# A conformer block on one core: whole chunks instead of half chunks behind the last exponential, and a newly searched order

## The chip, the cores and the metric

The kernel runs on one core of one Trainium2 chip. The metric is the time of one execution in device microseconds (us); lower is better. TensorE multiplies matrices, ScalarE evaluates activations, VectorE does elementwise work and reductions, GpSimd small elementwise work, and SyncE (SP) issues DMAs, as does ScalarE's queue now and then.

## What is computed

Two sequences of 4000 tokens with 144 features, bfloat16, go through one block. `_layernorm` has no weights.

```python
h = _layernorm(x); h = _silu(h @ w_ff1a) @ w_ff1b; x = x + 0.5 * h      # 144 -> 576 -> 144
h = _layernorm(x); qkv = h @ w_qkv                                       # 4 heads of 36
scores = jnp.einsum('bhqd,bhkd->bhqk', q, k) * scale; p = _softmax(scores)
x = x + (p @ v, heads merged) @ w_o
h = _layernorm(x) @ w_pw1; a, b = h[..., :D], h[..., D:]; h = a * _sigmoid(b)
c = depthwise convolution of h over tokens, 5 taps, w = dw
x = x + _silu(c) @ w_pw2
h = _layernorm(x); h = _silu(h @ w_ff2a) @ w_ff2b; x = x + 0.5 * h
return _layernorm(x)
```

The attention is over all 4000 tokens of a sequence: 2 x 4 x 4000 x 4000 exponentials. The rest is linear in the tokens.

## The kernel before

**Tiling.** The 8000 tokens are 16 chunks of 500, chunks 0 to 7 being the first sequence; a chunk is four blocks of 125 tokens. The keys of a chunk's queries are walked in tiles of 64 (63 per sequence, the last one of 32 rows). One item is one key tile for one chunk and all four heads: 16 x 63 = 1008 items. TensorE makes the scores in four 64x64 quadrants into two PSUM banks, an engine takes the exponential into a tile `PT`, and TensorE multiplies `PT` with the values `VA` (37 columns, the last one of ones, so that the sums come along). `TYPES` says per item who takes the exponential: `A` ScalarE in one instruction of 1000 columns, `D` VectorE in two of 500 by integer arithmetic on the bits and three more steps, `W` the same with one first instruction of 1000 columns, `R` the short last tile on ScalarE.

**Stages of a chunk.** `pre` is the first feed-forward and the projections. `epilogue` normalises the attention's sums into `AN`. `post1` transposes `AN`, adds the projection by `w_o`, and makes layer norm and gated unit (`U`). `post2` makes the convolution (`conv`, `conv_left`) with its SiLU (`SW`), the projection by `w_pw2`, a layer norm with transposes (`ln_tr`), the second feed-forward (`ff` for whole chunks, `ff_part` for half ones), the last layer norm and the store (`store`, which calls `ln` and issues the DMA to `out`).

**Half and whole chunks.** The function `small(c)` says whether chunk `c` goes in halves of two blocks:

```python
def small(c):
    return mode["tail"] or mode["front"] and c < FULL
def parts(c):
    return [range(0, 2), range(2, 4)] if small(c) else [range(0, 4)]
```

`mode["tail"]` is switched on when all items' exponentials and sums have been planned; the stages planned behind that point are called the tail here. They are `post1` of chunk 15 and `post2` of chunks 11 to 15. In `ln_tr` a half chunk is transposed by TensorE (four transposes of 125 columns for two blocks into a PSUM bank, then `copy` to `XTB`), a whole one by one DMA transpose that SP issues (`dma_transp`). In `ln`, a half chunk takes its variance step on VectorE by default, the power of -0.5 on GpSimd over 2 columns and the normalisation `XN` on VectorE or ScalarE; a whole one takes variance, power over 4 columns and `XN` on GpSimd by default. In the tail the SiLU is one activation on ScalarE: for a half chunk two of 500 columns (two tiles of 250 each) and one of 250, for a whole one four of 500 and one of 250. Chunks 14 and 15 share the convolution's seam at their end (`glu_end`, `conv_end`), which works on halves.

**The order.** A planner (`Sched`, `pick`, and in the tail a loop that takes the thread with the earliest start, shifted by `TJ`; `FLEX` shifts the choice of engine for copies) makes a list of steps. Its order is not the one that runs. `settle` and `arrange` put each engine's steps into the order of the table `ORDER` (steps numbered per engine, two letters each), and take the PSUM banks, the `PT` buffers and the places of the other PSUM tiles from `BANKS`, `SLOTS` and `PLACES`. `UNITS` holds one letter for each choice of engine among VectorE (`d`), GpSimd (`p`) and ScalarE (`a`), in the planner's order: copies, the variance step, the `XN` steps of a layer norm, and residual additions (on ScalarE these need two more matmuls with an identity). 465 letters before; the first 377 are planned ahead of the tail, and the first 106 of them within the front, where the first sequence's keys are made. Each engine runs its own list in order, and waits where a step needs another engine's result. All instructions are issued by one helper, so every row of the profile has its line, L591.

Of the kernel before, what the change touches and what calls it, by code (L numbers as in the profile page):

```python
# [13 lines left out]
H = 4  # L14
# [21 lines left out]
        '!!!#!$!%!&!(!)!*!+!,!-!.!/!0!1!2!5!4!7!3!6!<!8!9!=!:)n)o!;!>)r)s!?)v)w)z){!@!A*!*#!B!C*&*(!D*,*+!E!F'  # L36
        '!K!G!H!I!N!J!L!M!Q!S!R*$*.)|)u*))q*-)})x*%)p)y)t!V!T!W!U!P!b!O!`!^!X!Y!Z!_!j!a![!h!i!c!d!g!f!l!e!k!]'
        '*0*/!o!m*4*3!n!p*8*7*2***<*;!q*?*@*6*5*D*C*1*:!r!s*H*G!u*L*K!t!w!v*E*F*P*O*T*S!x!y*B*M*W*X!z*J*I*A*]'
        '*b*c*9*N*[*Q*>*f*g!{*k*j*Y*R!|!}*n*o###!*r*_*y*x*s*p*e*=*}*^*|*V*U*q#$#%#&+-+%+$*Z*a*z*v+.*{+)+**`*h'
        '*i*d+7+8#(+3+4*u+&#)+F+++2*t*l*w+;+<#*+E+(+#+!*m+?+0+/+I+J+:+Q+1+,+9+@+M+N+G+=+>#,#++R+W+X+O+]+L+P+6'  # L40
        '+[#-+`+f+C+g+K+5+D+_+a+^+k+j+Z+A#.+n+o+B+U+H+Y+V+v+r+s+T+S+|+}#/,%,$+m+l+i+u+t,),*+w+h,#,!+p,.,-#0,2'
        ',1#1,<,;+q,/+e+d,5,0,?,@,6+b+c,3,4+z,D,C#2,G,H,B,>,=,R,&,Q+{,K,F,+,L+y,E,U,V,J,A,:+x,,,I,Z,Y,_,S,9,^'
        ',T#3,c,b,8,7,W,X,f,(,l,m#4,p,q,[,g,d,P,e,M,t,u#5#6,y,x,],O,a,|-&-(#7-,-+,k,v,N,j,},r-0-/#8-4-3-.,z,w'
        ',`-7,{-=->#9-A-B-8-)-2-5---*-F-E-6-I,h,s-J-1#:-C-M-N,o,n-D-H-Q-R-V-U,i-K-G-<-]-[-$-@-!-%-`-a-O-e-d-P'
        '-9-#-j-k-T-S-L-;-:-?-o-n#=-r-s#;#<#?#@#>-v-w-Z-Y-{.&-z-_-^-c-l-u-m-b.!.##A#B#C.(-t...-#D.2.1.$.%-q-p'
        '-W-X.5.6#E-y.=-x.0.9.:#F.C.D.3.8./.4.7.>.H.G#G.K.L-f.<.,.;.+-i.P.O#H-|.S.T.X.N.W.F-g.M.?.Q.].E.R.[.V'
        '.A.@.`.c.*.B.i.j.Z.Y.m.n-}.I-h.J.^._.d.U.r.q.).b.a.u.v#I/#/$#J.p/(.o.f/).y.h.k/,/-/%.t#K.z/0.x.e.s/1'
        '/4.g/5/+/&.w.l/*/8///?/>#L/B/C.}/!/2/9/./F/G#M/J/K#N/U/T/N/E/I/H/A/6/D/Y/X/7/3/@/O/L.|#O/^/]/M/V/Z/b'
        '/a/=.{/W#P/j/</i/[/f/R/e/S/;/_/o#Q/y/x/`/|/:/}/g#R0$0%/Q/k/l/c/d/r0/00/m/n/s/P0304/h0)/q/p0=0>#S070A'
        '0B02010E0!0(0F08050&0#/z0*0O0P0C0@0?/{060I0T0S0G0H#T0W0X0D0Q0R0J0[0]#U0`0a0Y#V0d0e0^0Z0_/v0<0;0o0n/w'  # L50
        '0b090V0U0:0r0s/t0c/u0h0w0f0g0v#W0{0z0p0M0q0K0i1!1#0.0L0t0N0x1&1(#Y#X1+1,0-0,0|0}1%1/1$0u1)10#Z191:1-'
        '1*0y130m0+1=1>#[1B1A1.0l140j1F1E#]1I1J#^1N1M#_1U1R1H1Q1G1D17111]1[120k1C1?1V1<151;1`1a#`#a161O1e1S1Z'
        '1d1Y1_1@1W1i1h181^1l1X1m1s1r1L1T1K1b1c1v1w#b2%2$1z1k1f1g2*2)#c2.2-1n2(1j1{27281q2&2,211o2;2<1P201p22'
        '2?2@#d2+2J2I291y1u1t2C2#2/2B2>2M2N2:1|#e2Q2R2L2D2O1x2P2]2[262!2V2=2a2`242U1}2S2T2d2e#f2i2^2c2h2b2K2_'
        '2H2l2m232A#g2F2w2E2p2k2q252j2x#h2t3!2}2Z2n2r2Y2W2X3&3%2g3.2s2G2f3/3*3+2o2v2u3534#k#j39383,3-3=3<#i3A'
        '3@373(3)2{3;3L3E3D3M3:363?3H3I3#2|2y2z3B333R3S#l3V3W3F3G3>3$3K3_3[3Z3J3`3T3O323f3e313P3U303i3j3Y3q#m'
        '3n3]3m3N3r3x3k3w3l3^3C3h3X4(3Q3|3{#n3o4$4#433p3c3y4/3u3d4.3g3z3}4!423v4B4)#o#p48493b4<3s4&4M4%4L413a'
# [2435 lines left out]
```

## Time and profile before

| | |
|---|---|
| time, median of 3 runs | 875.51 us (875.36 to 875.64) |
| profiled execution, its own time | 875.88 us |
| its span, first to last instruction | 874.0 us |
| granted TensorE clock, mean | 0.998 |
| end of the last exponential | about 825.7 us of the span |

A profile row of a group has its engine, operation, output and inputs, shapes, count, busy time and mean duration; then the idle time of the engine just before such instructions and what ended it. A matmul's duration includes the latency of its pipeline, so that matmuls overlap; the time from one start to the next says how fast they go. A window's row has busy time by engine (count of instructions), then the granted clock.

### The profile page before, as it was taken

The numbers are of one execution on the slowest core, as the hardware profiler recorded it, in microseconds if no ns is written. First come the engines' busy times: TensorE is split into PE (matmuls) and PEld (weight loads), VectorE is DVE, ScalarE is ACT, GpSimd is POOL, SyncE is SP. The second block draws the span as 40 slices with busy tenths as digits, with TensorE's granted clock in tenths as the row PEclk, the third lists the DMA queues.
The fourth block names the chain that finished last, engine by engine and source line by source line (L and its number), as shares of the span: only waits on it lengthen the run. The fifth ranks groups of instructions, "written<-read, shape, count | busy, mean of one in ns | idle before, by whom it ended". The sixth has DMA issues, their size and how long they took to land.

```text
span 874.0 us, 27149 instructions
## 1 busy us (share of the span) xinstructions
PE 855.2 (98%) x11637; PEld 413.3 (47%) x11637; DVE 843.6 (97%) x1853; ACT 839.0 (96%) x1101; POOL 283.4 (32%) x540
## 2 busy tenths in 40 slices
PE   9999999999999999999999999999999999999996
PEld 7643434444344444434444444444545444444586
DVE  7999999999999999999999999999999999999987
ACT  7899999999999999999999999999999999999975
POOL 6760341031514302511330241210541260501645
PEclk9999999999999999999999999999999999999999
DMA  3230111102112101211310010101120021000201
GB/s 101 65 74 4 33 20 38 33 14 44 21 38 43 34 14 21 45 25 26 33 38 1 9 38 9 26 14 14 26 51 5 18 44 26 19 16 14 42 19 40
DMA packets 83552, 26.12 MB, mean 30 GB/s; under 512 B 78231, under 2 KB 83432, under 8 KB 83432
## 3 DMA queue, kind: packets, MB, share of 16 engines
q1 hardware_dynamic: 81884, 23.70, 14.2%
q8 instruction: 91, 1.49, 0.7%
q10 hardware_dynamic: 1548, 0.69, 0.3%
q14 instruction: 29, 0.24, 0.1%
HBM read 3.31 MB, written 2.30 MB: 6 GB/s over the span
## 4 chain that ended last, share of the span: by engine, by line
PE 43%; ACT 38%; DVE 16%; DMA 1%; issue 1%; POOL 1%; DVEq 0%; POOLq 0%; ACTq 0%
PE PS L591 43%; ACT PT L591 35%; DVE PT L591 11%; ACT TH L591 3%; DVE ST L591 1%; DMA XTB<-XN 1%; DVE U L591 1%; DVE X L591 1%; DVE XN L591 1%; DVE HT L591 0%; DVE QT L591 0%; DVE SW L591 0%; POOL XN L591 0%; DVE AN L591 0%; ACT KT L591 0%
## 5 line engine op out<-in xcount | busy, mean ns | idle before, releaser
L591 ACT ACTIVATE PT<-PS 128x1000 bf16<-128x1000 f32 (+1 forms) x793 | 731.4, 1071 | 6.2 <-PE PS L591 4.8
L591 PE MATMUL PS<-QT,KT 64*64 64x500 bf16 x3968 | 455.8, 383 | 4.3 <-ACT PT L591 1.2
L591 PE MATMUL PS<-PT,VA 64*37 64x500 bf16 x4828 | 451.9, 372 | 1.8 <-DVE QT L591 0.9
L591 DVE TENSOR_SCALAR PT<-PS 128x500 int16<-128x500 f32 (+1 forms) x424 | 279.9, 678 | 4.5 <-PE PS L591 2.5
L591 PEld LDWEIGHTS PS<-QT,KT 64*64 64x64 bf16 x3968 | 138.4, 104 | 203.8 <-ACT PT L591 103.3
L591 PEld LDWEIGHTS PS<-PT,VA 64*37 64x37 bf16 x4828 | 162.8, 96 | 107.1 <-DVE PT L591 15.0
L591 POOL TENSOR_SCALAR RS<-ST 125x4 f32<-125x4 f32 (+1 forms) x118 | 31.3, 266 | 484.6 <-DVE ST L591 480.2
L591 DVE TENSOR_SCALAR PT<-PT 128x1000 uint16<-128x1000 uint16 x430 | 171.5, 415 | 1.7 <-PE PS L591 0.5
L591 DVE TENSOR_TENSOR PT<-PT 128x1000 bf16<-128x1000 bf16 x215 | 145.4, 679 | 1.1
L591 POOL TENSOR_SCALAR XN<-X,RS 125x144 bf16<-125x144 bf16 x236 | 134.9, 585 | 3.9 <-DMA out_dram<-XN 0.3
L591 POOL TENSOR_TENSOR RS<-RS,NHALF 125x4 f32<-125x4 f32 (+2 forms) x99 | 97.0, 983 | 70.0 <-DVE RS L591 67.8
L591 ACT ACTIVATE TH<-PS 128x500 bf16<-128x500 f32 (+3 forms) x175 | 94.5, 564 | 3.4 <-PE PS L591 2.9
L591 DVE SCALAR_TENSOR_TENSOR HT<-TH,PS 128x500 bf16<-128x500 bf16 (+1 forms) x120 | 71.7, 614 | 1.8 <-ACT TH L591 1.0
L591 PE MATMUL PS<-XTB,WA 72*128 72x500 bf16 (+2 forms) x304 | 72.3, 344 | 0.5
L591 DVE BATCH_NORM_STATS2 ST<-X 125x6 f32<-125x288 bf16 (+1 forms) x160 | 66.2, 447 | 2.0 <-DMA X<-in_x_dram 1.1
L591 DVE SCALAR_TENSOR_TENSOR X<-PS,X 125x288 bf16<-125x288 f32 (+1 forms) x112 | 50.0, 450 | 4.1 <-PE PS L591 3.2
L591 PE MATMUL PS<-WB,HT 128*125 128x144 bf16 (+1 forms) x640 | 51.9, 229 | 0.1
L591 PEld LDWEIGHTS PS<-WB,HT 128*125 128x125 bf16 (+1 forms) x640 | 44.8, 136 | 12.7 <-issue 3.6
L591 PEld LDWEIGHTS PS<-XTB,WA 72*128 72x128 bf16 x304 | 23.0, 97 | 27.8 <-issue 9.5
L591 PE MATMUL PS<-U,DG 128*128 128x375 bf16 (+5 forms) x204 | 27.9, 263 | 0.1
L591 ACT ACTIVATE HT<-PS 128x500 bf16<-128x500 f32 (+3 forms) x46 | 21.4, 525 | 4.1 <-PE PS L591 3.6
L591 PE MATMUL PS<-IDF,QT 128*125 128x128 f32 x128 | 22.4, 298 | 0.1
(95 smaller groups left out, 525.1 us busy)
## 6 DMA issues: line engine op xcount, KB each, us to landing
X<-in_x_dram SPq DMA_DIRECT2D x16, 140.6 KB
XTQ<-XTB SPq DMA_DIRECT2D x24, 70.3 KB
out_dram<-XN SPq DMA_DIRECT2D x11, 140.6 KB
XTB<-XN SPq DMA_TRANSPOSE x50, 3.1
out_dram<-XN SPq DMA_DIRECT2D x6, 70.3 KB
XTB<-AN SPq DMA_TRANSPOSE x15, 3.1
out_dram<-XN ACTq DMA_DIRECT2D x3, 70.3 KB
WA<-in_w_ff1a_dram ACTq DMA_DIRECT2D x1, 144.0 KB
```

What stands on the lines that cost most here:

```text
L591: ins = getattr(eng, o.name)(*o.a, **o.k)
```

## The change

`small` is true in the tail for chunks 14 and 15 alone, so `post2` of chunks 11 to 13 goes whole: transposes by DMA, `ff` in place of `ff_part`, one layer norm of four blocks where there were two of two, one store of 140 KB where there were two of 70. GpSimd's memsets of constants at the start are tied into one step (`clears`). The tables of the order are replaced, `TJ` and `FLEX` too.

```diff
+    zero = R.step
+
+    def clears(eng, dst, w, cost):
+        was = R.step
+        if eng == "pool":
+            R.step = zero
+        op(eng, "memset", dst, 0.0, w=w, cost=cost)
+        R.step = was
...
-    op("pool", "memset", WP2Z[:, :, :], 0.0, w=[("WP2Z", i) for i in range(NB)], cost=0.3)
-    op("pool", "memset", U2[:, :, :], 0.0, w=["U20"], cost=0.6)
+    clears("pool", WP2Z[:, :, :], [("WP2Z", i) for i in range(NB)], 0.3)
+    clears("pool", U2[:, :, :], ["U20"], 0.6)
...
     def small(c):
-        return mode["tail"] or mode["front"] and c < FULL
+        return mode["tail"] and c >= 14 or mode["front"] and c < FULL
...
-    FLEX = -0.2
+    FLEX = 0.8
```

The memsets of `WE1`, `WB1`, `WE2`, `WB2`, `WQ` and `WK` become `clears` in the same way; those on VectorE keep their step. The tables in numbers:

| table | before | after |
|---|---|---|
| steps of TensorE, ScalarE, VectorE, GpSimd, SP | 5060, 1093, 1721, 314, 99 | 5049, 1083, 1691, 323, 99 |
| `TYPES` A, D, W, R | 777, 209, 6, 16 | 777, 211, 4, 16 |
| `UNITS` d, p, a | 289, 118, 58 | 264, 132, 51 |

`PLACES`, `BANKS` and `SLOTS` have the same places for 1543 of some 1725 tiles, 1803 of 2016 banks and 912 of 2016 buffers. The tables' letters themselves are left out.

More of the change, by code (lines that the diff above doesn't have):

```diff
@@ L41 @@
[L41 to L45, printed above, removed]
@@ new lines @@
+    '2402403540225042502240525042504250240124120412402140204120412041240214022425055240240420542054250520'
+    '5240420342034034203420342034202430243034303430342034204330340234203402550520420424042504205240524052'
+    '5042505230524052402240524045205425042504250524052402505250525052042405240025402540523054205420452305'
+    '2340324302430134033430343024301343024302430243024302432034203423024302430041204120412041204120420402'
+    '1402041204021402041204021402041204023402140245042054250425042045240240142010524025025024012041201402'
@@ new lines @@
+    '4522500134124500234523452300452345231145234523451111543401235401235501230154230123012301223401450145'
+    '0145012245014501450145220145014532014522014501324501452201450132450145014501222401230145230123014501'
+    '3223012345012301552301235201550155440123012301230155230123540123012354012301234401340144230123012301'
+    '2344500123452355012301340124340123450134015334014501453312452201450145014533124533014501334501450133'
+    '4501450133450145330145014501220145124523004523450023452345231045234500234523004523452300452345002345'
@@ new lines @@
+    '2300452345001245234545012344012301230123440123012301235510452345230123012301234500234500234523452345'
+    '0123452345231145234523114523452311451245234510234523452301452345234511234523452311050345123422014501'
+    '3345014522014501450133450132450145220145013345014525014501323401552301442301230123012301230123540123'
+    '0123013355012301442301234401234401230144230123015523012345012301234501230123015523012345012301443401'
+    '2355012301235401230155230123012344002345234510234523004523452311452345121035234523004523452301452345'
@@ new lines @@
+    '0132450145012345014532014523134512450312450123452345234523110345124512004512452201450133451245320145'
+    '0122450145013245014501453201450145332345234500124512034512453323452311451345235423451125450145013245'
+    '0134230145124532014501235201340123451023451203450145013245014522014501234501453301450125340145014501'
+    '4512452045001423012301230123250134012301452301230155230125430101234501452301452300452345012345234523'
+    '4500231045234523450145320145123401054401234523450023452303452345123345124501134523450110452345231145'
@@ new lines @@
+    ')!#!+,*!(!%!!!()&!*!-!#!,!$&%!!!+!-!,&(!*!)!%!#!!-$!),+!,!&!!&*!(!-#$!%!(!*+#!+!%!,!$!%!),&!$!,!%!(!'
+    '&!#!!!-%+!(!*!#!$!!!,!)*&!#!(!+!#-&!%!*$,!$!!!-()!&!,!+(#!)!$!&%!!)!#!$!-!!!*!+)$!,!-!#(%!!!&!*!-!+!'
+    ',$)!&!!!*#+!%!)!(!$!&!%!,$-!#*&!(&)-%!!!&!*!+!#!!!),%!*!+!*(-!%!$!&!!-#!+!%!#!,!$!($&!%!#!*!+!-!&!#!'
+    ')!)!*+,!$!(!&!!-%!)!,!$!#!*(%!,!)!-%&!,!#!+!&!$!#!)!*!(-$!,!#%!!&!$!*!!!+!)&$!,!*,-!%!(!#+!!&!+!$!)!'
+    '-!(!&!-!,&+!%!$!%##!+!-!)!(!-!+(*!)!&!%!*($!!!,!#&-!%!&!)!+!!(,!$!*!+*%!,!$!#!-!%!&!,!(,)!-!$!*$!!)!'
@@ new lines @@
+    '-!#(&!%!+!!&$),!+!%+*!-!#!&,+!)!(!-!$!!!)+#!%!-!(!$!!!,!%(!!*!,-#!+!)!&!$!%!#!(!$*+!)!,!#!&!+!%!-!+!'
+    '#&)!*!$!%!,!(+#!)!!!#!-%$!&!,!$!*+)!%!#!$-*!&(+!!!)!%!#!$(+!-!,!!!*!)-%!!!#!(!*!&!+)$%,!-!!!*$(!#!&!'
+    ')%,!(!-!#,!!,!&!-!,!+&-!!!*,(!%!!!)$-!(!!!%-#!-!&!!$+!)!#!(+*!)!*%-!&!#(,!!!)!$!,!+!&!)!!!-!$!(&+!,!'
+    '*!$!!!-!#*%!,!$!(!!!&!)!%$+!-!(-)!+!*!&-,!#!)!$!*&#!,!+!),!!$!%!(!#!$!+!-!(!!!$-%!(!)!,#*!+!$%-+&!+!'
+    '!!#)*!(!&!)!*-%!!!$!(,+!-!$!&!!!,!#&%!+!!!)!*,(!-!%!$&)!+!#!!!(*)!,!#!)!#+&$,!(!-!),*!%!!!,!$&-!+!(!'
@@ new lines @@
+    '-!%(*!+!#!)!,+!!*!(!$%)!#!-!+)&!%!#!&%$!(!,!!!-!*!%!-!#!*!&!)+$!!!%!-!(&#!*!,!+)$!*!,!%#-!*!$!#$!!,!'
+    ')!*)&!(!+!-!!($!+!,!&!%!)*+!$!&!,!(-+!%!!!$!#&,!*!+!%!$!)!+!,&-!$!#!!*+!(-)!$!%,+!)!#!%,&!-!,!(!!+#!'
+    '$!&!*$)!#!(!+!!#-!(!)!+!&*,!-!%!)!-!,+$!(!#!!)*!(!)!%!-$+!*!#!,+&!+!$!(-!!+!*!%)$!&!(!$!*!%!#!(!&!-!'
+    ')!*!&!$%+!,!!*#!(!)!&!+!-!%-*,$!,!#!(!)!+-!!&!$!#!!)&!(!*-%&)!-!(+$!,!#!+!)$,!-!-+!!$!&!#!!!*!&!%!(!'
+    ',!*-+!%$$!&!!!+!(!&!#!!,)!+!(!)!#!-(&!&!+!*!,!%!($)!-!#!*$)!!!%!-!%!)!,!+!!!())!+!,!*!$++!#!-!&!,(-!'
@@ L299 @@
+    'ddadppdadppdddddppppdddpdppdddddadddddppadadppddddpadppdddddddpdddadppdadappddpddppddddppdppdddppddp'
+    'pdddppddpddppddappdddppdppddddppdppddppddppddppdddddppdpdddaapppdddaadppdppppddpppdddddaaddddpddddpd'
+    'pddpppdddadddaddddddddpddpddadpadddddddaddddddd'
 )
@@ L1090, in bass_standalone__conformer_family_zipformer__speech_kernel @@
     for WE, WB, nm, eng in ((WE1, WB1, "W1", "dve"), (WE2, WB2, "W2", "pool")):
-        op(eng, "memset", WE[0:HD, :, 0:64], 0.0, w=[(nm, "a", 2)], cost=0.15)
-        op(eng, "memset", WE[0:HD, :, 128:192], 0.0, w=[(nm, "a", 3)], cost=0.15)
+        clears(eng, WE[0:HD, :, 0:64], [(nm, "a", 2)], 0.15)
+        clears(eng, WE[0:HD, :, 128:192], [(nm, "a", 3)], 0.15)
         op("dve", "memset", WB[64:128, 4, :], 0.0, w=[(nm, "b", 3)], cost=0.15)
-        op(eng, "memset", WB[0:64, 5, :], 0.0, w=[(nm, "b", 4)], cost=0.15)
-    op("pool", "memset", WQ[:, :, :, :], 0.0, w=["WQ0"], cost=0.3)
-    op("pool", "memset", WK[:, :, :, :], 0.0, w=["WK0"], cost=0.3)
+        clears(eng, WB[0:64, 5, :], [(nm, "b", 4)], 0.15)
+    clears("pool", WQ[:, :, :, :], ["WQ0"], 0.3)
+    clears("pool", WK[:, :, :, :], ["WK0"], 0.3)
     op("dve", "tensor_copy", IDF[:, :], IDENT[:, :], r=["ID"], w=["IDF"], cost=0.2)
```

429 lines of the change are left out of this document (197 added, 232 removed), and 24 rows, old and new, of the table TJ.

## The prediction

> **What bounds the kernel now.** I read the page's sums first, then the busy time of each engine by stage, then the chain of waits, the timeline of TensorE, and the groups by form.
>
> ```profile
> span 874.0 us, 27149 instructions
> PE 855.2 (98%) x11637; PEld 413.3 (47%) x11637; DVE 843.6 (97%) x1853; ACT 839.0 (96%) x1101; POOL 283.4 (32%) x540
> ```
>
> Three engines look full, so the sums alone cannot say what a change is worth. The stages can. The columns are the stretch, its length, and then busy us of PE, PEld, DVE, ACT and POOL:
>
> ```profile
> 0.00:60.00 60.00, 57.54 (x707) 38.79 (x707) 53.02 (x150) 49.31 (x89) 44.20 (x91) 1.00 0.32 81
> 60.00:826.00 766.00, 757.42 (x10468) 339.51 (x10462) 751.32 (x1573) 757.73 (x942) 215.04 (x402) 1.00 0.14 25
> 826.00:866.00 40.00, 39.00 (x457) 34.03 (x456) 35.30 (x118) 30.64 (x69) 21.38 (x45) 1.00 0.14 33
> 866.00:874.00 8.00, 1.24 (x17) 0.94 (x14) 3.92 (x16) 1.35 (x3) 2.80 (x4) 0.74 0.19 54
> ```
>
> From 60 to 826 (the attention) ScalarE and VectorE carry the exponentials and leave 8.3 and 14.7 us idle. Behind the last exponential, 826 to 866, ScalarE idles 9.4 us of 40 and VectorE 4.7, but TensorE only 1.0. Its busy time is partly modelled latency, so I check the chain and the spacing of its instructions:
>
> ```profile
> 828.11 4.72 DMA XTB<-XN
> 832.83 0.05 issue
> 832.88 28.88 PE PS L591 x344
> 861.76 0.00 issue
> 861.76 2.74 PE PS L591 x34
> ...
> 868.60 1.14 DVE XN L591 x5
> ```
>
> ```profile
> 862.62 1.01 PE L591 MATMUL PS<-XTB,WA 72*128 72x250 bf16 x8
> 863.47 0.39 PE L591 MATMUL PS<-IDENT,XN 125*72 125x125 bf16 x4
> 863.70 0.79 PE L591 MATMUL PS<-WB,HT 128*125 128x144 bf16 x10
> 864.32 0.59 PE L591 MATMUL PS<-XTB,WE 72*128 72x250 bf16 x4
> ```
>
> The chain is one unbroken run of 378 matmuls, 31.6 us, behind one wait of 4.72 us for a DMA transpose. The second fence shows that it is not only latency: each group starts as the one before has streamed. Eight 250-column matmuls take 0.85 us to the next group (106 ns each), four transposes 0.23 (58 ns each), ten 144-column matmuls 0.62. So in this stage TensorE's own work sets the end, and then comes a drain of some 8 us led by VectorE and the last store.
>
> **The change, part by part.** These are the rows with the prices in the tail (826 to 874):
>
> ```profile
> L591 PE MATMUL PS<-IDENT,XN 125*72 125x125 bf16 x44 | 4.3, 218 | 0.0
> L591 PE MATMUL PS<-IDENT,XN 126*72 126x126 bf16 x4 | 0.4, 217 | 0.0
> L591 DVE COPY XTB<-PS 72x500 bf16<-72x500 bf16 x8 | 3.3, 412 | 2.5 <-PE PS L591 2.3
> L591 ACT ACTIVATE XTB<-PS 72x500 bf16<-72x500 bf16 x5 | 2.9, 585 | 0.7 <-PE PS L591 0.6
> L591 ACT ACTIVATE HT<-PS 128x500 bf16<-128x500 f32 x26 | 14.3, 585 | 2.7 <-PE PS L591 2.6
> L591 ACT ACTIVATE HT<-PS 128x250 bf16<-128x250 f32 x11 | 4.1, 379 | 1.1 <-PE PS L591 1.0
> L591 DVE TENSOR_SCALAR RS<-ST 125x2 f32<-125x2 f32 x13 | 2.1, 163 | 0.3
> L591 POOL TENSOR_TENSOR RS<-RS,NHALF 125x2 f32<-125x2 f32 x20 | 14.2, 713 | 14.3 <-DVE RS L591 13.8
> L591 POOL TENSOR_TENSOR RS<-RS,NHALF 125x4 f32<-125x4 f32 x2 | 2.1, 1049 | 0.8 <-DVE RS L591 0.8
> ```
>
> *Transposes.* 48 transposes of XN are six layer norms of 8: one in `post1` of chunk 15, one in `post2` of each of chunks 11 to 15. Going whole takes 3 x 8 = 24 from chunks 11 to 13, at 58 ns of stream: **1.4 us off TensorE**, on the chain. With them go 6 evacuations (0.41 us on VectorE or 0.59 on ScalarE, about 3.0 us together), off the chain as long as both engines have room.
>
> *Feed-forward.* A half chunk has two SiLUs of 500 columns and one of 250; two halves cost 4 x 0.585 + 2 x 0.379 = 3.10 us of ScalarE, a whole chunk 4 x 0.585 + 0.379 = 2.72. Three chunks save 1.1 us, hidden in ScalarE's 9.4 us of idle time. TensorE's columns stay (20 matmuls of 250 become 8 of 500 and 4 of 250): nothing.
>
> *Layer norms.* Each chunk has two in this stage. Whole ones need one power of 1.05 us where two of 0.71 stood, and one variance step where two of 0.163 stood. VectorE gains 6 x 0.163 = 1.0 us, GpSimd 6 x 0.38 = 2.3, both beside TensorE. VectorE leads the last 5 us of the drain, so I put 0.3 us of all its relief on the end; between nothing (these chunks are done by then) and 1.0.
>
> *DMA transposes.* SP gets three more transposes in the tail and three stores fewer (two 70 KB stores become one of 140), so its number of steps stays 99. What a transpose makes wait is seen here, behind a layer norm on GpSimd:
>
> ```profile
> 815.99 2.87 POOL L591 TENSOR_SCALAR XN<-X,RS 125x144 bf16<-125x144 bf16 x4
> 822.34 0.45 PEld L591 LDWEIGHTS PS<-XTB,WPZ 72*128 72x128 bf16 x8 [0.34 <-DMA XTB<-XN]
> 832.87 0.22 PEld L591 LDWEIGHTS PS<-XTB,WE 72*128 72x128 bf16 x3 [1.20 <-DMA XTB<-XN]
> PE PS L591 <- DMA XTB<-XN: 0.9, 1, 0.9
> ```
>
> From the last XN (818.86) to the reader's start are 3.5 us, in the chain above 4.7; TensorE stood still for 0.9 of it at 832. Queued behind such a wait is all of TensorE, in order, and behind it ScalarE's SiLUs. Three more cost between nothing (other chunks' convolutions, projections and feed-forwards fill the time, as they nearly do here) and 3 x 0.9 = 2.7 us. There are five chunks to interleave and three of them need it early, so I take 0.3. It could also gain the 0.9 that stands there now, if the new order covers it. [...]
>
> *Clears.* GpSimd's memsets are tied into one early step. They already run there, in one go, and GpSimd then waits for VectorE, so I put nothing on it; without that gap a power of 1.4 us would come later by what is left of them.
>
> ```profile
> 3.45 0.52 POOL L591 MEMSET WK<- 128x512 bf16 x1
> 5.56 1.39 POOL L591 TENSOR_TENSOR RS<-RS,NHALF 125x2 f32<-125x2 f32 x2 [1.59 <-DVE RS L591]
> ```
>
> *The order of everything else.* This is the unknown. The tables show what moves: of 1008 key tiles the kinds of 8 change, with 777 on ScalarE as before, VectorE's wide form `W` 6 to 4 and its split form `D` 209 to 211. Of the 377 choices of engine planned ahead of the tail (the first letters of `UNITS`; the first 106 belong to the front) I counted the changed letters. Beyond the front: residuals 5 each way, the copies of QT, KT and VA balanced, 6 more variance steps and one more whole XN (four steps) on GpSimd instead of VectorE.
>
> ```profile
> L591 DVE TENSOR_SCALAR PT<-PS 128x500 int16<-128x500 f32 x418 | 272.8, 670 | 4.5 <-PE PS L591 2.5
> L591 DVE TENSOR_SCALAR PT<-PS 128x1000 int16<-128x1000 f32 x6 | 7.1, 1191 | 0.0
> L591 DVE TENSOR_SCALAR XN<-X,ST,RS 125x144 bf16<-125x144 bf16 x72 | 19.6, 337 | 0.5 <-POOL RS L591 0.3
> L591 POOL TENSOR_SCALAR RS<-ST 125x4 f32<-125x4 f32 x100 | 27.4, 275 | 480.9 <-DVE ST L591 477.5
> L591 POOL TENSOR_SCALAR XN<-X,RS 125x144 bf16<-125x144 bf16 x236 | 134.9, 585 | 3.9 <-DMA out_dram<-XN 0.3
> ```
>
> VectorE: 2 x (2 x 0.670 - 1.191) = +0.3, -6 x 0.163 = -1.0, -4 x 0.337 = -1.3: together -2.0 us of 751. ScalarE: nothing. GpSimd: +6 x 0.275 + 4 x 0.585 = +4.0, with 70% of it idle. The work of this stage is the same within 0.3%; only gaps can move it. ScalarE's 8.3 us of gaps bound a gain; a loss has no such bound, and I take ScalarE's gaps at half as much again, 4.2 us, as its far end. I take -0.5, a quarter of VectorE's relief, because ScalarE is the fuller engine. For the front (TensorE 57.5 of 60) I take nothing, within 1 us either way.
>
> *Sum:* -1.4 - 0.3 + 0.3 - 0.5 = -1.9. The profiled execution took 875.88 us (span 874.0 and 1.9 around it): 874.0. The median of the runs is 0.4 lower, 875.51, so I forecast **873.6 us**, -0.22%. About 0.2% (1.75 us) is what a measurement of this kernel can tell from no change.
>
> **The rivals.**
>
> *The new order closes gaps as well.* If half of ScalarE's 8.3 us goes too, 3.6 us come on top of the 0.5 taken: 870.0. For it: VectorE is relieved and every table is new. Against it: the stage is 98.9% busy on ScalarE already.
>
> *The transposes by DMA take the gain back.* All three stall TensorE as the one at 832 does: 2.7 instead of 0.3, so 876.0, no change. Against it: the wait exists once among the many readers of that stage.
>
> *GpSimd blocks VectorE.* More steps on GpSimd may delay VectorE. VectorE's multiply of two tiles, with GpSimd nearly idle (60 to 80) and with it busy (240 to 260):
>
> ```profile
> L591 DVE TENSOR_TENSOR PT<-PT 128x1000 bf16<-128x1000 bf16 x4 | 2.7, 675 | 0.1
> L591 DVE TENSOR_TENSOR PT<-PT 128x1000 bf16<-128x1000 bf16 x5 | 3.5, 694 | 0.0
> ```
>
> 19 ns more, 3%. If VectorE stood for half of the 4.0 us that GpSimd gains, its relief of 2.0 and my 0.5 would be gone: 874.1 or, with the tail's layer norms on GpSimd too, up to 875.0. [...]
>
> *Slower: gaps on ScalarE in the attention.* TensorE's queue is in order, and a score pair that stands behind a sum still waiting for its exponential holds up the next one. Place: 60 to 826. Before, ScalarE waits little for TensorE:
>
> ```profile
> ACT PT L591 <- PE PS L591: 4.8, 20, 0.6
> ```
>
> The new sequence of TensorE has little in common with the old one (the longest common run of steps covers 32%), so these 20 waits are drawn anew. The price is that of the gaps: 4.2 us give 873.6 + 0.5 + 4.2 = 878.3. It decides once ScalarE's gaps grow by over 3.2 us (8.3 to 11.5), which eats the tail's 1.4 and leaves 1.75.
>
> **How the numbers follow.** Forecast (872.2 to 875.2): 0.52, of which 0.38 falls under 873.75 and 0.14 above. Gaps closed: 0.15. Transposes: 0.08. GpSimd: 0.05. Slower: 0.20. So faster 0.53, same 0.27, slower 0.20. The range cuts half of the slower case and little of the case of closed gaps: 869.9 to 877.9.
>
> **What would show it.** TensorE's transposes of XN by 24 fewer, DMA transposes 53 instead of 50; TensorE's run from the last exponential to its last matmul (826 to 866) shorter by 1 to 2 us; no wait of TensorE for XTB over 1 us; ScalarE's idle time from 60 to the tail within 2 us of 8.3. The prediction is wrong if the tail keeps its 48 us, or if the last exponential ends more than 2 us earlier or later.

## The result, and the profile after

The changed kernel takes **872.24 us** (median of 6 runs, 871.45 to 872.35) where the kernel before, in runs beside it, took 875.58 (6 runs, 875.07 to 876.19): a ratio of 0.9959, 95% interval 0.9946 to 0.9971, 3.3 us faster. Its profiled execution took 872.24 us, 3.64 less than that of before. The page's sums after:

```profile
span 870.4 us, 27016 instructions
PE 850.9 (98%) x11585; PEld 409.6 (47%) x11585; DVE 837.1 (96%) x1824; ACT 834.7 (96%) x1093; POOL 284.4 (33%) x562
```

(The helper that issues all instructions is line L589 in the changed kernel, and one of L589 to L593 in the kernels of the experiments.) Three engines are as full as before, so the sums again don't say where 3.6 us went. Three stretches do, cut where the last exponential ends and where the last matmul ends. The busy time by stage, first of the kernel before, then after (columns as in the prediction):

```profile
60.00:825.68 765.68, 757.10 (x10466) 339.39 (x10460) 751.00 (x1571) 757.73 (x942) 214.72 (x402) 1.00 0.14 25
825.68:867.34 41.66, 40.56 (x474) 35.09 (x470) 36.96 (x123) 31.09 (x70) 22.70 (x47) 1.00 0.14 34
867.34:874.00 6.66, 0.00 (x0) 0.00 (x0) 2.58 (x12) 0.90 (x2) 1.79 (x3) 0.69 0.17 49
```

```profile
60.00:823.49 763.49, 755.13 (x10451) 339.61 (x10448) 749.55 (x1569) 756.66 (x941) 211.87 (x414) 1.00 0.14 26
823.49:861.47 37.98, 37.98 (x431) 30.87 (x428) 32.27 (x102) 28.62 (x65) 21.98 (x43) 1.00 0.24 52
861.47:870.40 8.93, 0.00 (x0) 0.00 (x0) 3.28 (x13) 0.00 (x0) 1.71 (x2) 0.65 0.16 48
```

So the last exponential ends 2.2 us earlier (825.68 to 823.49), TensorE's stretch behind it is 3.7 us shorter (41.66 to 37.98), and the drain behind the last matmul is 2.3 us longer (6.66 to 8.93). -2.2 - 3.7 + 2.3 is -3.6, the whole difference.

**TensorE's stretch.** It was 1.10 us short of full and is now full (37.98 of 37.98), and its work has shrunk. The groups by form from 823.49 to the end, and the DMA issues:

```profile
L589 PE MATMUL PS<-IDENT,XN 125*72 125x125 bf16 x20 | 1.9, 219 | 0.0
L589 PE MATMUL PS<-IDENT,XN 126*72 126x126 bf16 x4 | 0.4, 218 | 0.0
...
XTB<-XN SPq DMA_TRANSPOSE x53, 3.2
```

Of 48 transposes by TensorE 24 are left, and three more go by DMA. The wait for a DMA transpose at 832 is gone. The two orders also divide other work differently: behind the last exponential 65 matmuls of the convolution (`PS<-U,DG`) stand where 72 stood, and 20 sums with `PT` where 6 did. What this shift is worth, beside the wait and the transposes, was not measured by itself. SP's timeline of after shows the two transposes before the tail:

```profile
819.70 1.23 SPq L589 DMA_TRANSPOSE XTB<-XN  x1
822.28 0.28 SPq L589 DMA_DIRECT2D out_dram<-XN  x1
825.44 1.23 SPq L589 DMA_TRANSPOSE XTB<-XN  x1
```

In the kernel before the last two were issued at 826.6 and 828.1 and first read at 830.8 and 832.9, with TensorE standing still for the second. Now they go 6.9 and 2.7 us earlier; the first is read at 825.2, 5.5 us behind its issue, and from 820 to 866 the view of waits has none of TensorE for `XTB`.

**The drain.** SP's and ScalarE's queues and the last windows of after:

```profile
858.07 6.09 SPq L589 DMA_DIRECT2D out_dram<-XN  x3
863.52 1.63 ACTq L589 DMA_DIRECT2D out_dram<-XN  x3
```

```profile
860.00:864.00 4.00, 1.47 (x24) 1.32 (x22) 3.53 (x13) 0.97 (x3) 2.42 (x3) 1.00 0.04 14
864.00:868.00 4.00, 0.00 (x0) 0.00 (x0) 0.85 (x4) 0.00 (x0) 0.00 (x0) 0.52 0.30 89
```

The last column is GB/s. From 860 to 864 almost nothing is moved (14, the end of an earlier store), then 89 GB/s for 4 us, which is 356 KB, and some 75 KB more in the next microsecond: two whole chunks' stores and the halves of chunk 15 (422 KB in all) land together at the very end. The last `XN` steps on VectorE, in the kernel before and in the changed one:

```profile
868.51 1.45 DVE L591 TENSOR_SCALAR XN<-X,ST,RS 125x144 bf16<-125x144 bf16 x6
862.95 1.90 DVE L589 TENSOR_SCALAR XN<-X,ST,RS 126x144 bf16<-126x144 bf16 x8
```

They are done at 869.96 and 864.85. So the drain has two parts. From the last matmul to the last `XN` it took 2.6 us and takes 3.4: a whole chunk's last norm now stands among those of the two halves. From there to the end it took 4.0 us and takes 5.5. Of the 2.3 us, 0.8 are norms and 1.5 lie behind the last norm, where only stores are left.

**Ahead of the tail.** How much of the exponentials is done by 750 us: busy time on tile `PT` alone, from 60 to 750, of ScalarE (first row) and of VectorE (second row), in the kernel before and then in the changed one:

```profile
60.00:750.00 690.00, 640.75 (x696) 1.00 0.14 26
60.00:750.00 690.00, 499.74 (x953) 1.00 0.14 26
```

```profile
60.00:750.00 690.00, 642.76 (x698) 1.00 0.15 27
60.00:750.00 690.00, 501.92 (x958) 1.00 0.15 27
```

At 750 us both engines are 2.0 and 2.2 us of exponentials ahead, about what the last exponential's end moved by. The figure depends on the cut, since other work of ScalarE stands at other places: cut at 200, 400, 600, 700 and 800 us it is 0.6, 0.3, 0.9, 1.1 and 1.3 us ahead. So the lead gathers over the attention, for the most part behind 400 us, and not at one place. The front gives none of it: by 60 us ScalarE's exponentials came to 19.91 us before and 19.74 after. From 60 us to the last exponential ScalarE runs nearly the same work in both (942 and 941 instructions), so the 2.2 us are mostly gaps: 1.1 us of idle time (765.68 - 757.73 = 7.95 to 763.49 - 756.66 = 6.83), and 1.1 us of busy time. Overlapping instructions count once in it (in the kernel before, one of ScalarE's ends at 807.61 and the next starts at 807.38), so closer starts can show as less busy time; how much of the 1.1 us is that, and how much the one instruction less, was not taken apart.

### The profile page after: what moved, and what is told of

The parts are those of the page before. It is cut to its first block, busy times and chain, and to the rows that moved or that the text cites. A ratio compares the mean times of both kernels' runs of the same rounds, so it can differ in the third digit from the quotient of the medians.

```text
span 870.4 us, 27016 instructions
## 1 busy us (share of the span) xinstructions
PE 850.9 (98%) x11585; PEld 409.6 (47%) x11585; DVE 837.1 (96%) x1824; ACT 834.7 (96%) x1093; POOL 284.4 (33%) x562
## 4 chain that ended last, share of the span: by engine, by line
PE 50%; ACT 27%; DVE 20%; DMA 2%; issue 1%; POOL 1%; SPq 0%; DVEq 0%; POOLq 0%
PE PS L589 50%; ACT PT L589 24%; DVE PT L589 13%; ACT TH L589 3%; DVE ST L589 1%; DVE QT L589 1%; DVE HT L589 1%; DMA XTB<-XN 1%; DVE X L589 1%; DVE KT L589 1%; DMA XTQ<-XTB 1%; DVE SW L589 0%; POOL RS L589 0%; POOL XN L589 0%; ACT QT L589 0%
## 5 line engine op out<-in xcount | busy, mean ns | idle before, releaser
L589 ACT ACTIVATE PT<-PS 128x1000 bf16<-128x1000 f32 (+1 forms) x793 | 731.9, 1073 | 5.3 <-PE PS L589 4.2
L589 PE MATMUL PS<-QT,KT 64*64 64x500 bf16 x3968 | 452.5, 384 | 5.6 <-ACT PT L589 2.7
L589 PE MATMUL PS<-PT,VA 64*37 64x500 bf16 x4828 | 449.0, 372 | 1.3 <-DVE QT L589 0.3
L589 DVE TENSOR_SCALAR PT<-PS 128x500 int16<-128x500 f32 x426 | 281.0, 677 | 4.5 <-PE PS L589 2.5
L589 PEld LDWEIGHTS PS<-QT,KT 64*64 64x64 bf16 x3968 | 136.8, 104 | 207.0 <-ACT PT L589 101.3
L589 PEld LDWEIGHTS PS<-PT,VA 64*37 64x37 bf16 x4828 | 162.1, 96 | 103.6 <-issue 16.6
L589 POOL TENSOR_SCALAR RS<-ST 125x4 f32<-125x4 f32 (+2 forms) x132 | 34.1, 261 | 504.7 <-DVE ST L589 500.6
L589 DVE TENSOR_SCALAR PT<-PT 128x1000 uint16<-128x1000 uint16 x430 | 173.6, 419 | 2.1 <-PE PS L589 0.5
L589 DVE TENSOR_TENSOR PT<-PT 128x1000 bf16<-128x1000 bf16 x215 | 145.8, 682 | 0.9
L589 POOL TENSOR_SCALAR XN<-X,RS 125x144 bf16<-125x144 bf16 x250 | 141.6, 579 | 4.2 <-POOL RS L589 0.2
L589 ACT ACTIVATE TH<-PS 128x500 bf16<-128x500 f32 (+3 forms) x175 | 95.2, 569 | 5.3 <-PE PS L589 4.7
L589 POOL TENSOR_TENSOR RS<-RS,NHALF 125x4 f32<-125x4 f32 (+2 forms) x93 | 89.5, 973 | 23.5 <-DVE RS L589 20.9
L589 DVE SCALAR_TENSOR_TENSOR HT<-TH,PS 128x500 bf16<-128x500 bf16 (+1 forms) x120 | 72.5, 618 | 1.2 <-ACT TH L589 0.7
L589 PE MATMUL PS<-XTB,WA 72*128 72x500 bf16 (+2 forms) x280 | 71.6, 360 | 0.4 <-DVE PT L589 0.2
L589 DVE BATCH_NORM_STATS2 ST<-X 125x6 f32<-125x288 bf16 (+1 forms) x160 | 65.8, 449 | 2.9 <-DMA X<-in_x_dram 2.2
L589 DVE SCALAR_TENSOR_TENSOR X<-PS,X 125x288 bf16<-125x288 f32 x114 | 51.0, 452 | 5.1 <-PE PS L589 4.4
L589 PE MATMUL PS<-WB,HT 128*125 128x144 bf16 (+1 forms) x640 | 51.6, 229 | 0.0
L589 PEld LDWEIGHTS PS<-WB,HT 128*125 128x125 bf16 (+1 forms) x640 | 44.6, 136 | 12.6 <-issue 3.7
L589 PEld LDWEIGHTS PS<-XTB,WA 72*128 72x128 bf16 x280 | 20.8, 97 | 27.9 <-issue 10.6
L589 PE MATMUL PS<-U,DG 128*128 128x375 bf16 (+7 forms) x204 | 28.0, 263 | 0.1
L589 ACT ACTIVATE HT<-PS 128x500 bf16<-128x500 f32 (+3 forms) x43 | 20.2, 539 | 5.5 <-PE PS L589 5.3
L589 POOL COPY U<-U 128x2 bf16<-128x2 bf16 (+1 forms) x54 | 10.1, 225 | 45.9 <-DVE U L589 45.9
```

Source lines behind the costliest of these rows:

```text
L589: ins = getattr(eng, o.name)(*o.a, **o.k)
```

## The experiments

Each was timed in five rounds beside the kernel before, whose median beside them was 875.50 to 875.76. The theory: the gain is the new order ahead of the tail (2.2), TensorE's work and wait in the tail (3.7), less a drain that got longer (2.3). The rivals: the whole-chunk tail alone, or the order alone, carries all of it, and the drain is fixed time.

**The order of the last two stores.** In the changed kernel the store of chunk 13, whose `XN` is ready at 859.9, stands on SP behind half of chunk 15, ready at 863.5. The edit swaps these two steps, the last of `ORDER["sp"]`:

```diff
-        '!T!U!W!Y!X![!Z!]!^!`!a!e!b!_!f!c!g!h!i!d!m!j!o!l!n!p!k!q!r!t!s!u!v!y!|!z!}!w!{!x#!#%###&#$#(#*#+#)'
+        '!T!U!W!Y!X![!Z!]!^!`!a!e!b!_!f!c!g!h!i!d!m!j!o!l!n!p!k!q!r!t!s!u!v!y!|!z!}!w!{!x#!#%###&#$#(#*#)#+'
```

> The changed kernel with the last two steps of SP swapped: the store of chunk 13 goes ahead of that of chunk 15's second half, which waits for its layer norm until about 864. Theory: the drain behind TensorE's last matmul (8.9 us instead of 6.7) is long because three whole chunks' stores, 140 KB each, land together at some 95 GB/s; chunk 13's would leave four us earlier, into an idle stretch, and take 140 KB / 95 GB/s = 1.4 us off the end: about 870.9. Rival: the end is one DMA's fixed latency behind the last layer norm, whatever lies ahead of it: no change, 872.2.

Measured: 871.30 us (871.28 to 871.73), ratio 0.9954 (0.9942 to 0.9966). By the medians that is 0.9 us below the changed kernel, but the intervals of the two ratios overlap; the profile carries the reading. Its windows:

```profile
860.00:864.00 4.00, 1.49 (x24) 1.33 (x22) 3.51 (x13) 0.99 (x3) 2.41 (x3) 1.00 0.16 49
864.00:868.00 4.00, 0.00 (x0) 0.00 (x0) 0.87 (x4) 0.00 (x0) 0.00 (x0) 0.79 0.25 71
```

Chunk 13's data now moves in the idle stretch (14 to 49 GB/s), and the end comes 4.5 us behind the last `XN` instead of 5.5 (span 869.4). This is the fastest complete kernel of the study.

**Short stores.** The stores of chunks 11 to 13 write 32 of 125 rows, which leaves the rest of their output out and serves for timing alone, once with the order just shown and once with the changed kernel's own:

```diff
-                put(out_tok[c][:, b0:b1, :], XNC[0:TB, u, 0:n, :], u)
+                few = 32 if mode["tail"] and 11 <= c <= 13 else TB
+                put(out_tok[c][0:few, b0:b1, :], XNC[0:few, u, 0:n, :], u)
```

> The changed kernel with the store of chunk 13 ahead, and the stores of chunks 11 to 13 writing only 32 of their 125 rows (the rest of these rows is left unwritten). Theory (the last 4.5 us, from the last XN to the end, are in part the data of a whole chunk's store beside the halves of 15): 871.3 - 1.0 = 870.3 us. Rival, this stretch is the fixed time of the last small store: 871.3 us, no change.

> The same short stores, but the changed kernel's own order, in which the store of chunk 13 waits behind one half of 15. Theory (the 0.9 us that the order of stores was worth is chunk 13's data arriving beside the others): 872.2 - 1.3 = 870.9 us or below. Rival (it is the store's place in the queue, not its data): 872.2 us, no change.

Measured: 869.73 us (869.30 to 870.41), ratio 0.9932 (0.9920 to 0.9945), and 869.67 us (869.00 to 869.99), ratio 0.9929 (0.9916 to 0.9943). The last windows of the second:

```profile
864.00:868.00 4.00, 0.00 (x0) 0.00 (x0) 0.79 (x4) 0.00 (x0) 0.00 (x0) 0.82 0.19 55
868.00:874.00 6.00, 0.00 (x0) 0.00 (x0) 0.00 (x0) 0.00 (x0) 0.00 (x0) 0.84 0.01 1
```

Same instructions and order as the changed kernel, 220 KB instead of 356 from 864 to 868, and 2.6 us off; the last `XN` is done at 864.8 as before and the span ends 3.0 us behind it. With little data the place in the queue no longer matters (869.73 and 869.67). The rival of fixed time falls: here the last matmul ends at 861.4 and the drain is 6.4 us instead of 8.9, so 2.5 of it are data of whole chunks. That is not the same as the 2.3 by which the drain grew: the norms' 0.8 us are in the 2.3 and stay in this run (861.4 to 864.8), and its stores land faster (3.0 us behind the last `XN`) than those of the kernel before (4.0).

**Transposes twice.** In the kernel before, the 24 transposes by TensorE that the change removes are issued twice:

```diff
-                          [("XT", s, i) for i in bs], len(bs), rows)
+                          [("XT", s, i) for i in bs], len(bs), rows, 2 if mode["tail"] and 11 <= c <= 13 else 1)
...
-                    ins = getattr(eng, o.name)(*o.a, **o.k)
+                    for _ in range(getattr(o, "rep", 1)):
+                        ins = getattr(eng, o.name)(*o.a, **o.k)
```

> The kernel before, with each of the 24 TensorE transposes of chunks 11 to 13 in post2 of the tail issued twice (same result, no step or wait added). Theory: TensorE's own work sets the end of this stage, so 24 x 58 ns = 1.4 us more of it come out whole: about 877.0. Rival: waits of the layer norms set it and TensorE has slack: within 0.4 us of 875.6.

Measured: 876.67 us (median of 12; 875.97 to 881.43), ratio 1.0017 (1.0007 to 1.0026): +1.2 us, or 49 ns for each transpose. TensorE's own work sets the end there, as the theory has it. The one profiled execution is the 881.43, and it shows something else:

```profile
830.00:832.00 2.00, 1.44 (x16) 0.90 (x13) 1.93 (x7) 0.96 (x3) 0.41 (x1) 1.00 0.36 91
832.00:834.00 2.00, 1.46 (x10) 0.95 (x11) 1.71 (x6) 0.94 (x3) 1.43 (x4) 1.00 0.00 0
834.00:836.00 2.00, 2.00 (x11) 1.19 (x10) 0.10 (x1) 1.82 (x5) 0.52 (x1) 0.52 0.00 0
836.00:838.00 2.00, 2.00 (x12) 1.56 (x11) 1.29 (x6) 0.61 (x3) 1.01 (x5) 0.50 0.00 0
```

Behind the pause at the late DMA transpose (0.56 + 0.54 us idle) TensorE was granted half its clock for 10 us; the other 11 runs end at 877.41 or below.

**New order, old tail.** The old kernel's plan with half chunks; each engine runs the changed kernel's order until the last scores, then the old one. All five tables of order change; of `ORDER["sp"]`:

```diff
-        '!!!#!%!&!(!$!)!*!+!,!-!.!/!0!1!2!3!5!4!6!7!9!:!<!8!=!>!?!@!B!;!A!D!E!F!G!C!H!I!J!K!L!O!Q!N!M!R!P!S!V'
-        '!T!U!W!X!Y![!Z!]!`!^!_!a!e!b!f!g!h!c!i!m!j!d!k!o!n!l!p!q!r!t!u!v!s!y!w!|!z!}!{!x#!#$###%#&#(#+#)#*'
+        '!!!#!%!&!(!$!)!*!+!,!-!.!/!0!1!2!4!3!5!6!7!9!:!<!=!8!>!?!@!B!A!;!D!C!E!F!G!H!J!I!K!L!O!Q!M!R!P!N!S!V'
+        '!T!U!W!Y!X![!Z!]!^!`!a!e!b!_!f!c!g!h!i!d!m!j!o!l!n!p!k!q!r!t!s!u!v!y!|!z!}!w!{!x#!#$###%#&#(#+#)#*'
...
```

> The kernel before (half chunks in the tail), with the order, the engines and the places of the changed kernel for all steps that it has begun by the end of the scores, and those of the kernel before for the rest. Theory: the part ahead of the tail and the tail are worth 2.2 and 1.4 us independently: 875.6 - 2.2 = 873.4, plus what the seam costs. Rival 1: only the tail's whole chunks bring something: 875.6. Rival 2: the new order only moved work out of the tail or into it, and is worth nothing without the new tail: 875.6 or more, with the last exponential as early as 823.5 and a longer tail.

Measured: 874.37 us (873.98 to 875.00), ratio 0.9989 (0.9980 to 0.9997), -1.1. ScalarE's timeline:

```profile
818.15 5.21 ACT L591 ACTIVATE PT<-PS 128x500 bf16<-128x500 f32 x6
824.99 0.59 ACT L591 ACTIVATE QT<-PS 128x500 f32<-128x500 f32 x1 [1.64 <-PE PS L591]
825.60 1.28 ACT L591 ACT_TABLE_LOAD   x1
```

The last exponential ends at 823.36, as early as in the changed kernel, so that gain needs no whole chunk. But the seam loses 1.64 us before `QT`, and half of it is gone.

**Old order, new tail.** The complement: the changed kernel's plan, the old order until the last scores. Against the changed kernel, of `ORDER["sp"]`:

```diff
-        '!T!U!W!Y!X![!Z!]!^!`!a!e!b!_!f!c!g!h!i!d!m!j!o!l!n!p!k!q!r!t!s!u!v!y!|!z!}!w!{!x#!#%###&#$#(#*#+#)'
+        '!T!U!W!X!Y![!Z!]!`!^!_!a!e!b!f!g!h!c!i!m!j!d!k!o!n!l!p!q!r!t!u!v!s!y!w!|!z!}!{!x#!#%###&#$#(#*#+#)'
...
```

> The changed kernel (whole chunks 11 to 13), with the order, the engines and the places of the kernel before for all steps that it has begun by the last scores, and the new ones for the rest. Theory: the tail alone brings 1.4 us: 874.2, plus what the seam costs, with the last exponential at 825.7. Rival: the gain is all ahead of the tail: 875.6. If this and the kernel with the new order and the old tail add up to 3.4 us of gain, the two parts are independent.

Measured: 880.42 us (878.42 to 881.25), ratio 1.0056 (1.0044 to 1.0068). It says nothing on the tail, since its seam stops TensorE:

```profile
822.00:824.00 2.00, 0.06 (x4) 0.06 (x8) 1.93 (x5) 0.83 (x1) 0.36 (x1) 1.00 0.00 0
824.00:826.00 2.00, 1.43 (x13) 0.32 (x14) 2.00 (x5) 0.00 (x0) 0.81 (x3) 0.57 0.00 0
826.00:828.00 2.00, 2.00 (x13) 1.02 (x11) 1.70 (x5) 0.46 (x2) 1.89 (x3) 0.50 0.00 0
```

A pause of 2 us, and then half the clock until about 831.

**Seams further ahead.** Four more such splices, at two earlier places, the new order first (against the kernel before) or the old order first (against the changed one):

```diff
 ORDER["sp"], new order to item 878 (about 750 us), against the kernel before
-        '!T!U!W!X!Y![!Z!]!`!^!_!a!e!b!f!g!h!c!i!m!j!d!k!o!n!l!p!q!r!t!u!v!s!y!w!|!z!}!{!x#!#$###%#&#(#+#)#*'
+        '!T!U!W!Y!X![!Z!]!^!`!a!e!b!_!f!c!g!h!i!d!m!j!o!l!n!p!k!q!r!t!u!v!s!y!w!|!z!}!{!x#!#$###%#&#(#+#)#*'
...
 ORDER["sp"], old order to item 880, against the changed kernel
-        '!T!U!W!Y!X![!Z!]!^!`!a!e!b!_!f!c!g!h!i!d!m!j!o!l!n!p!k!q!r!t!s!u!v!y!|!z!}!w!{!x#!#%###&#$#(#*#+#)'
+        '!T!U!W!X!Y![!Z!]!`!^!_!a!e!b!f!g!h!c!i!m!j!d!k!o!n!l!p!q!r!t!s!u!v!y!|!z!}!w!{!x#!#%###&#$#(#*#+#)'
...
```

The other two differ from the same two kernels in the first row of `ORDER["sp"]` alone, and likewise in the early part of the other lists.

> The changed kernel's order for the steps of the first 750 us or so, then the old order for the rest, with 11 to 13 as half chunks and the old tail. Theory (the gain ahead of the last exponential, 2.2 us, is gathered evenly by the order of attention, and the tail's 1.4 us is apart from it): 875.5 - 2.0 = 873.5 us, and up to 1 us more if the seam leaves a gap. Rival, the gain ahead of the tail comes only from the last 75 us, where the new order has put off less work: 875.5 us. Rival, it all comes early, from the first half: 873.3 us.

> The complement: the old order for the first 750 us, then the new order for the rest, whole chunks and the new tail. Theory (even gain): 875.5 - 1.4 - 0.2 = 873.9 us, up to 1 us more with a gap at the seam. Rival (last 75 us alone): 872.2 us. Rival (all of it early): 874.1 us. If 5 and this one together gain much less than 3.4 us without gaps at the seams, order and tail don't add up and each needs the other.

> The new order for the first half of the steps alone, then the old order and the old tail. Theory (even gain): 875.5 - 1.0 = 874.5 us. Rival, the gain lies in the last 75 us: 875.5 us. Rival, all of it in the first half: 873.3 us.

> The old order for the first half of the steps, then the new order with the new tail. Theory (even gain): 875.5 - 1.4 - 1.2 = 872.9 us. Rival, last 75 us alone: 872.2 us. Rival, all of it in the first half: 874.1 us.

Measured, in this order: 874.65 us (ratio 0.9987, 0.9979 to 0.9996), 875.17 (0.9993, 0.9984 to 1.0002), 877.76 (1.0036, 1.0022 to 1.0051) and 873.85 (0.9980, 0.9971 to 0.9989). ScalarE's timeline shows the seam of the second, third and fourth, a row each:

```profile
729.02 0.59 ACT L590 ACTIVATE PT<-PS 128x500 bf16<-128x500 f32 x1 [0.80 <-PE PS L590]
```

```profile
391.33 0.59 ACT L591 ACTIVATE VA<-PS 128x504 bf16<-128x504 f32 x1 [1.26 <-PE PS L591]
```

```profile
387.17 1.00 ACT L589 ACTIVATE PT<-PS 128x1000 bf16<-128x1000 f32 x1 [1.21 <-PE PS L589]
```

Only the first splice has a clean seam. It gains 1.1 us, its last exponential ends at 824.84 (0.8 earlier), and at 750 us ScalarE is 1.3 us of exponentials ahead:

```profile
60.00:750.00 690.00, 642.05 (x697) 1.00 0.15 26
```

That excludes the rival by which the order gains only in the last 75 us. It leaves 1.4 of the 2.2 us to steps that this splice gave back or never had. The third, expected at 874.5 and measured at 877.76, missed by more than any theory had: the pieces of the order within the attention don't add up. That each is right only behind its own past is the reading; no run shows it by itself.

**The first fifth alone.**

```diff
 ORDER["sp"], new order to item 117, against the kernel before
-        '!!!#!%!&!(!$!)!*!+!,!-!.!/!0!1!2!3!5!4!6!7!9!:!<!8!=!>!?!@!B!;!A!D!E!F!G!C!H!I!J!K!L!O!Q!N!M!R!P!S!V'
+        '!!!#!%!&!(!$!)!*!+!,!-!.!/!0!1!2!4!3!5!6!7!9!:!<!=!8!>!?!@!B!;!A!D!E!F!G!C!H!I!J!K!L!O!Q!N!M!R!P!S!V'
...
```

> The changed kernel's order for the first fifth of the steps alone (about the first 170 us), then the old order, old half chunks and old tail. Theory (the 1 us that the new order gains ahead of 750 us is one stretch, 60 to 200 us, where ScalarE's idle time falls from 1.7 to 0.7 us): 875.6 - 0.9 = 874.7 us, unless the seam leaves a gap, which the profile would show. Rival (the gain is spread evenly to 750 us): 875.4 us.

Measured: 877.01 us (876.02 to 877.16), ratio 1.0013 (1.0004 to 1.0022). Inconclusive: ScalarE stands still at the seam for longer than the gain in question.

```profile
139.41 1.00 ACT L591 ACTIVATE PT<-PS 128x1000 bf16<-128x1000 f32 x1 [1.45 <-PE PS L591]
```

**The two parts, read apart.** A splice that lost time at its seam still tells what each part is worth, for the last exponential's end (`PT` on ScalarE) and the span cut its profiled execution in two. The rows with that end in the splices with the old order to item 435 and to item 880:

```profile
820.36 5.22 ACT L589 ACTIVATE PT<-PS 128x500 bf16<-128x500 f32 x6
821.77 5.22 ACT L590 ACTIVATE PT<-PS 128x500 bf16<-128x500 f32 x6
```

| kernel | chunks 11 to 13 | last exponential's end | span | from there to the end |
|---|---|---|---|---|
| before | halves | 825.68 | 874.0 | 48.3 |
| new order to item 117 | halves | 826.77 | 875.0 | 48.2 |
| new order to item 440 | halves | 828.50 | 876.6 | 48.1 |
| new order to item 878 | halves | 824.84 | 873.1 | 48.3 |
| changed | whole | 823.49 | 870.4 | 46.9 |
| old order to item 435 | whole | 825.58 | 872.3 | 46.7 |
| old order to item 880 | whole | 826.99 | 873.7 | 46.7 |

(The two splices behind the last scores have their seam within the last column, and are left out.) With whole chunks the time from the last exponential on is 46.7 to 46.9 us, with half chunks 48.1 to 48.3, whatever order stood ahead and wherever the last exponential ended. So the tail is worth about 1.5 us by itself, the 3.7 less the 2.3 from above: the old order to item 435 has its last exponential where the kernel before has it, and is 1.9 us faster (873.85 to 875.73). The order ahead is worth what it moves the last exponential's end by, and the two add. The rivals by which either part carries all of the gain are excluded.

**The late norm, earlier.** One thing that the new order does, done alone in the old one: the `XN` steps behind the transpose that TensorE waited for go to GpSimd, and their transpose goes first.

```diff
-    'pdddppdppdadpddappdddppdppddddppddpddppddppdddpdddddppdpddddddpppaadaddpdpddddaddddpdddddddddddadddd'
+    'pdddppdppdadpddappdddppdppddddppddpddppddppdddpdddddppdpddddddpppaadaddpdppdddaddddpdddddddddddadddd'
...
-        '!T!U!W!X!Y![!Z!]!`!^!_!a!e!b!f!g!h!c!i!m!j!d!k!o!n!l!p!q!r!t!u!v!s!y!w!|!z!}!{!x#!#$###%#&#(#+#)#*'
+        '!T!U!W!X!Y![!Z!]!`!^!_!a!e!b!f!g!h!c!i!m!j!d!k!o!n!l!p!q!r!t!u!v!s!y!w!|!z!{!}!x#!#$###%#&#(#+#)#*'
```

> The kernel before, with one step moved: the layer norm whose transpose TensorE waits for at 832.9 us (four XN steps of VectorE at 827.1, though its power is done at 822.1) goes to GpSimd directly behind that power, and its DMA transpose goes ahead of the one issued at 826.6. Nothing else changes. Theory (in the old order TensorE lost 0.9 to 1.2 us to that late transpose, and the new order gains it by issuing its transposes earlier): 875.5 - 0.9 = 874.6 us, and no wait of TensorE for XTB over 0.3 us in 826 to 836. Rival, TensorE then waits as long for something else: 875.5 us. Rival, the norm holds GpSimd against the next power (823.7) and delays the other transpose: up to 876.5 us.

Measured: 876.07 us (875.48 to 877.40), ratio 1.0006 (0.9997 to 1.0014): no gain. GpSimd's, VectorE's and TensorE's timelines tell why:

```profile
822.39 2.79 POOL L591 TENSOR_SCALAR XN<-X,RS 125x144 bf16<-125x144 bf16 x4
...
826.21 1.22 DVE L591 TENSOR_SCALAR XN<-X,ST,RS 125x144 bf16<-125x144 bf16 x4 [0.73 <-POOL RS L591]
...
828.08 0.70 PE L591 MATMUL PS<-IDF,QT 128*125 128x128 f32 x4 [1.11 <-DVE QT L591]
```

The wait for `XTB` is gone, and 1.11 us for `QT` stand in its place: the four steps hold GpSimd for 2.79 us, the next power comes later, VectorE waits 0.73 us for it, and `QT`, queued behind that norm on VectorE, is late for TensorE. Both rivals hold. The new order has neither wait, so it moved more than this one norm; which of its moves were needed was not tested.

## Why the prediction was right, and where its steps were not

The forecast was 873.6 us, faster by 1.9; measured are 3.3, inside its range. That a shorter tail and an earlier last exponential bring the gain is what the runs show; the sizes are another matter. The terms, against the two profiled executions:

*Transposes on TensorE, -1.4: right.* 24 are gone, and 24 more cost 1.2 us.

*Waits for DMA transposes, +0.3, "between nothing and 2.7": the sign was wrong.* None of the three new ones makes TensorE wait, and the old wait went too, 0.9 to 1.2 us, a case that the text named and did not take. Wait and transposes make 2.1 to 2.6 of TensorE's 3.7 us; the rest lies in other work that the two orders place differently, for which the sum has no term, and it was not measured by itself. So TensorE's run got shorter by more than the "1 to 2 us" that the text gave as a sign. In the old order the late transpose took 4.8 us from issue to reader (828.11 to 832.88), and the new order covers it by an earlier issue (819.70 for a reader at 825.2).

*The drain, -0.3, bounds 0 and -1.0: the step that failed most.* It counted VectorE's relief in the layer norms and noted that two stores of 70 KB become one of 140, but gave the data no price. It costs +2.3, outside its bounds. 0.8 of that are the norms themselves, which got longer behind the last matmul and not shorter, and 1.5 are behind the last norm, where the stores of two whole chunks land with chunk 15's; short stores take off 2.6. The bounds knew VectorE's relief only.

*The order ahead of the tail, -0.5: mis-sized.* It is -2.2, past the mark at which the text itself calls the prediction wrong (the last exponential "more than 2 us earlier or later"). A quarter of VectorE's relief was the wrong measure; the lead is on both engines. The rival of closed gaps (3.6 us more) holds for its direction, at less than half its price.

So the drain was 2.6 us worse than forecast and TensorE's stretch 2.6 us better, which cancelled, and the order's 1.7 us is what the sum missed. That the time fell inside the range is in part luck. Of the other rivals, that of GpSimd was not put to the test: from 60 us to the last exponential its busy time fell (214.72 to 211.87) instead of rising by 4.0. VectorE's multiplies of two tiles take 145.4 us in all before and 145.8 after, but its 430 `uint16` steps 171.5 and 173.6, a difference whose cause is open. A slower order on ScalarE is what the splices show, with single waits of 0.8 to 1.6 us drawn anew by each, so its place and kind of price were right, but the changed kernel's own order has no such wait. ScalarE's idle time, foretold within 2 us of 8.3, is 6.83.

Open stay two things. Which steps of the new order make the lead is not settled, because every splice within the attention but one waits at its seam for as long as the gains that it was to measure. And the whole-chunk tail was not run without any of the new order: it has its 1.5 us behind the old order up to item 880, so it needs at most the last 75 us of the new one, but the splice behind the last scores lost 2 us and the clock at its seam.

## What to carry to other kernels

When small stores are merged near the end of a kernel, price their data against what else must land after the last instruction, and issue each as soon as its data is ready: here the data of whole chunks, two of which landed behind the last norm, cost some 2.5 us, more than the 24 transposes save (1.2). A wait on the critical engine need not go when the one step that ends it is moved (1.11 us for `QT` stood in place of 0.9 to 1.2 for `XTB`): here the engine to which it was moved owed something to the next wait. A splice of two orders is a poor stopwatch, since all but one of them waited anew at the seam; cut its profile where one part ends, and each part can be read by itself.

## What the hardware showed

A short pause of TensorE was followed by half its granted clock in two profiled executions, and in a third it was not. A pause of 2.03 us in the splice behind the last scores (above, 822 to 824) was followed by a granted clock of 0.57, 0.50 and 0.50; five of its six runs have a mean clock of 0.993 and took 880.18 to 881.25 us, the sixth 0.997 and 878.42. The pause with the transposes twice (0.56 and 0.54 us) was followed by 0.5 for 10 us, in a run of 881.43 us with a mean clock of 0.992; the other 11 have 0.997 to 0.999 and took 877.41 or less. A pause of 1.11 us in the kernel with the early norm was followed by no lower clock:

```profile
824.00:828.00 4.00, 2.96 (x35) 1.13 (x27) 3.23 (x9) 3.41 (x5) 4.00 (x7) 1.00 0.34 66
828.00:832.00 4.00, 3.92 (x45) 3.49 (x46) 2.59 (x9) 1.86 (x5) 0.39 (x3) 1.00 0.49 106
```

What decides whether the clock falls was not shown: pauses of 1.1 us stand on both sides.
